# The second expert stage: both inner tiles of a step in one run, the last step's second product in one run, and two blocks' input split on another engine

## The chip, the core and the metric

The kernel runs on one core of a Trainium2 chip. The core has five engines with a queue each: TensorE (PE; matmuls, with the loads of the stationary operand shown apart as PEld), VectorE (DVE), ScalarE (ACT), GpSimd (POOL), and SyncE (SP), which here issues the DMAs. An engine works through its own queue in order and waits on semaphores for the others. The metric is the device time of one execution in microseconds (us), as the median over runs.

## What is computed

Three parts follow one another: a decayed linear attention, a mixture of eight experts, and a dense layer with a cosine gate. The change touches the third, for 3072 tokens of width 384 and an inner width of 2048:

```python
def _moe2_ref(x, w_in, w_out):
    h = x @ w_in
    g = h * np.cos(h)
    return (g @ w_out).astype(np.float32)
```

`x` is what the experts put out. The kernel treats the dense layer as a second expert stage.

## The kernel before

The tokens are cut into six blocks of 512 (`tb` 0 to 5). The inner widths are cut into units of 256: 32 units for the eight experts (`u` 0 to 31) and eight for the dense layer (`u` 32 to 39). A **step** is one unit on one block; the outer loop runs over units, the inner one over blocks. A unit has two inner tiles of 128 (`f` 0 and 1).

For precision every operand is held as a rounded high part and the rest: `xh`, `xl` for the input, `wh`, `wl` for the weights, `hh`, `hl` for the inner activations. A product is then three matmuls (`three`, lines 294 to 297): high by high, high by low, low by high.

A step has a first product for each inner tile (`g1`: nine matmuls of 512 columns, "wide") and a second product. In the dense layer the second product (`g2`) makes four token tiles of 128 by 384, six matmuls of 384 columns ("narrow") each. In the first stage it is transposed (`g2T`) and made of wide matmuls too.

Between the products of the dense layer stands `cos_split`, for each inner tile: ACT writes an Identity with an added constant (line 320), DVE subtracts (321), ACT does Sin (324) and Square (325), DVE multiplies (`g`, 328), ACT rounds to `hh` (331), POOL subtracts to `hl` (332). The scratch of these operations is called `raw` in the trace. The last two are put into a list, `late`, and taken out by the next tile's `cos_split` between its subtraction and its Sin.

The order of TensorE's work is written out by hand. `step` makes one tile's first product, then takes one entry off the list `g2q`, which holds second products in halves of two token tiles. With `lag=1` in the dense layer one entry stays in the list, so that TensorE alternates there: nine wide, twelve narrow, nine wide, twelve narrow. `one` advances a step by a quarter, and ahead of each quarter it advances the weight conversion (`wq`) and the input split (`xq`) by a piece.

`to_moe2` turns the experts' result of a block into the dense layer's input, in three pieces: ACT scales (662) and rounds to `xh` (663), POOL subtracts to `xl` (664). Blocks 0 to 3 are done in the last unit of the first stage, blocks 4 and 5 in steps 0 and 2 of unit 32. In that unit ACT also evacuates the second products (346); in the later ones DVE does (348). `ps` are the PSUM buffers: three rotate for first products, five for second ones.

Of the kernel before, what the change touches and what calls it, by code (L numbers as in the profile page):

```python
# [9 lines left out]
F32 = mybir.dt.float32  # L10
# [4 lines left out]
ALU = mybir.AluOpType  # L15
# [15 lines left out]
NU1 = E * UPE  # L31
NU2 = FF2 // FU
NU = NU1 + NU2
# [4 lines left out]
NTB = NT // TB  # L38
# [172 lines left out]
def body(tc, ap, t, fast, branch=None):  # L211
    nc = tc.nc
    te, act, dve, pool, sp = nc.tensor, nc.scalar, nc.vector, nc.gpsimd, nc.sync
    acc, accT, P, xh, xl = t.acc, t.accT, t.P, t.xh, t.xl
    wq, xq, gq = deque(), deque(), deque()

    class Ring:
        def __init__(self, items):
            self.items, self.n = list(items), 0
# [61 lines left out]
    def weight_tasks(u, loaded=False):  # L281
        if not loaded:
            load_w(u, 0)
            load_w(u, 1)
            yield
            for _ in range(1 if u < NU1 else 4):
                yield
        for i in range(NWP):
            yield from split_w(u, i)
            if 1 < u < NU1:  # L290
                yield


    def three(ps, ah, al, bh, bl, first, last):
        te.matmul(ps, ah, bh, start=first, stop=False)  # L295
        te.matmul(ps, ah, bl, start=False, stop=False)  # L296
        te.matmul(ps, al, bh, start=False, stop=last)  # L297
# [3 lines left out]
    def relu_split(e, tb, ps, hh, hl):  # L301
        if e:
            h = hring32.next()
            dve.scalar_tensor_tensor(out=h, in0=ps, scalar=0.0, in1=t.pb[tb], op0=ALU.max, op1=ALU.mult)  # L304
            act.activation(out=hh, in_=h, func=AF.Copy)  # L305

            def rest():
                dve.tensor_tensor(out=hl, in0=h, in1=hh.bitcast(F32), op=ALU.subtract)  # L308

            return rest  # L310
        act.activation(out=hh, in_=ps, func=AF.Relu)
        dve.scalar_tensor_tensor(out=hl, in0=ps, scalar=0.0, in1=hh.bitcast(F32), op0=ALU.max, op1=ALU.subtract)

    tring = Ring([t.raw[i][:, j * TB:(j + 1) * TB] for i in range(2) for j in range(2)])
    late = deque()

    def cos_split(ps, hh, hl):

        f = tring.next()
        act.activation(out=f, in_=ps, func=AF.Identity, bias=t.magic)  # L320
        dve.scalar_tensor_tensor(out=f, in0=f, scalar=MAGIC, in1=ps, op0=ALU.subtract, op1=ALU.subtract)  # L321
        if late:
            late.popleft()()
        act.activation(out=f, in_=f, func=AF.Sin, scale=math.pi)  # L324
        act.activation(out=f, in_=f, func=AF.Square)

        def g():
            dve.scalar_tensor_tensor(out=f, in0=f, scalar=0.5, in1=ps, op0=ALU.subtract, op1=ALU.mult)

        def split(last=False):  # L330
            act.activation(out=hh, in_=f, func=AF.Copy)  # L331
            (dve if last else pool).tensor_tensor(out=hl, in0=f, in1=hh.bitcast(F32), op=ALU.subtract)  # L332

        late.append(split)
        return g

    def evacT(u, tb, k, ps):
        a = accT[tb][:, k]
        if u == 0:
            act.activation(out=a, in_=ps, func=AF.Copy)  # L340
        else:
            dve.tensor_tensor(out=a, in0=ps, in1=a, op=ALU.add)  # L342

    def evac(u, tt, ps):
        if u == NU1:
            act.activation(out=acc[tt], in_=ps, func=AF.Copy, scale=TWO_PI)
            return
        dve.scalar_tensor_tensor(out=acc[tt], in0=ps, scalar=TWO_PI, in1=acc[tt], op0=ALU.mult, op1=ALU.add)
        if u == NU - 1:
            sp.dma_start(out=ap["out"][tt * 128:(tt + 1) * 128, :], in_=acc[tt])  # L350
# [3 lines left out]
    g2q = deque()  # L354

    def g1(u, tb, f):
        assert (u, 1) in wdone
        wh, wl = t.wh[u % 2], t.wl[u % 2]
        hh, hl = hid[u, tb, f] = hring.next()
        ps = ps1.next()  # L360
        for k in range(KT):
            o = k * FU + f * 128
            three(ps, wh[:, o:o + 128], wl[:, o:o + 128], xh[tb][:, k], xl[tb][:, k], k == 0, k == KT - 1)
        if u < NU1:
            return relu_split(u // UPE, tb, ps, hh, hl)
        return cos_split(ps, hh, hl)

    def g2_part(u, tb, i, f, ps):
        assert (u, 3) in wdone
        wh, wl = t.wh[u % 2], t.wl[u % 2]  # L370
        s = slice(i * 128, (i + 1) * 128)
        hh, hl = hid[u, tb, f]
        o = KT * FU + f * DM
        three(ps, hh[:, s], hl[:, s], wh[:, o:o + DM], wl[:, o:o + DM], f == 0, f == 1)

    def g2T(u, tb, k):
        assert (u, 3) in wdone
        wh, wl = t.wh[u % 2], t.wl[u % 2]
        ps = ps2.next()
        for f in range(2):  # L380
            hh, hl = hid[u, tb, f]
            o = KT * FU + f * DM + k * 128
            three(ps, wh[:, o:o + 128], wl[:, o:o + 128], hh, hl, f == 0, f == 1)
        evacT(u, tb, k, ps)

    def g2(u, tb, i):
        ps = ps2.next()[:, 0:DM]
        for f in range(2):
            g2_part(u, tb, i, f, ps)
        evac(u, tb * TPB + i, ps)  # L390

    def load_pb(e, tb):
        row = (e * NTB + tb) * TPB
        sp.dma_start(
            out=t.pb0[tb] if e == 0 else t.pb[tb],
            in_=t.pT[row:row + TPB, :].rearrange("t p -> (t p)").partition_broadcast(128))

    def step(u, tb, lag=0):

        if u == UPE:  # L400
            assert not gq
            pool.tensor_tensor(
                out=accT[tb], in0=accT[tb],
                in1=t.pb0[tb].rearrange("p (o n) -> p o n", o=1).to_broadcast([128, KT, TB]), op=ALU.mult)
        for f in range(2):
            rest = g1(u, tb, f)
            if f == 1 and u >= UPE and (u + 1) % UPE == 0 and u + 1 < NU1:
                load_pb((u + 1) // UPE, tb)
            yield
            if len(g2q) > lag:  # L410
                a, b, ks = g2q.popleft()
                for k in ks:
                    (g2T if a < NU1 else g2)(a, b, k)
                    if rest and u < NU1:
                        rest = rest()
            if rest:
                rest()
            if f == 1:
                g2q.extend([(u, tb, (0,)), (u, tb, (1, 2))] if u < NU1 else [(u, tb, (0, 1)), (u, tb, (2, 3))])
            yield  # L420


# [231 lines left out]
            load_pb(1, tb)  # L654
            load_pb(0, tb)

    def to_moe2(tb):

        yield
        for k in range(KT):  # L660
            a = accT[tb][:, k]
            act.activation(out=a, in_=a, func=AF.Copy, scale=1.0 / TWO_PI)  # L662
            act.activation(out=xh[tb][:, k], in_=a, func=AF.Copy)
            pool.tensor_tensor(out=xl[tb][:, k], in0=a, in1=xh[tb][:, k].bitcast(F32), op=ALU.subtract)
            yield


    dense = deque()

    def pull(q):  # L670
        while q:
            try:
                next(q[0])
                return
            except StopIteration:
                q.popleft()

    class Step:
        def __init__(self, u, tb, lag=0):
            self.it, self.left, self.u = step(u, tb, lag), 4, u  # L680

    def one():

# [48 lines left out]
    for c in range(NCH):  # L732
# [27 lines left out]
        if c == 2:  # L760
            act.activation(out=t.gater[:, :, 0:E], in_=t.gate, func=AF.Copy)
            dve.tensor_tensor(
                out=t.gater[:, :, E:2 * E], in0=t.gate, in1=t.gater[:, :, 0:E].bitcast(F32), op=ALU.subtract)
# [11 lines left out]
    for u in range(2, NU):  # L775
        if u == UPE:
            while gq:
                pull(gq)
            ps1.items.append(X0)
            ps2.items.extend([X1, X2])  # L780
        for tb in range(NTB):
            if tb == (1 if u + 1 < NU1 else 0) and u + 1 < NU:
                wq.append(weight_tasks(u + 1))
            if u == NU1 - 1 and tb >= 2:
                xq.append(to_moe2(tb - 2))
            if u == NU1 and tb in (0, 2):
                xq.append(to_moe2(NTB - 2 + tb // 2))
            if u == NU1 and tb == 4:
                assert not xq
            dense.append(Step(u, tb, lag=1 if u >= NU1 else 0))  # L790
            while one():
                pass

    late.popleft()(True)
    u, tb, ks = g2q.popleft()
    while len(g2q) >= 2:
        for i in ks:
            g2(u, tb, i)
        u, tb, ks = g2q.popleft()
    last = [ps2.next()[:, 0:DM] for _ in range(TPB)]  # L800
    for f in range(2):
        for i in range(TPB):
# [90 lines left out]
```

## Time and profile before

| | us |
|---|---|
| median of 3 runs | 2107.65 (2105.99 to 2108.02) |
| profiled execution, its own time | 2106.08 |
| its span | 2104.2 |
| TensorE busy | 2083.2 (99%) |
| DVE, ACT, POOL busy | 1357.3, 659.3, 484.1 |
| granted TensorE clock, mean | 0.997 |

The span is the time from the first to the last instruction of the profiled execution, whose own time is 1.88 us longer. A busy TensorE is not TensorE at its peak: the profile models the ends of its matmuls, so the distance between their starts is the better measure of its rate. A timeline row gives the start, the duration, the engine, the source line, the operation with what it writes and reads, and, in square brackets, how long the engine stood idle before it and what released it.

### The profile page before, as it was taken

How to read it: one execution, taken by the hardware profiler on the slowest of the kernel's cores; microseconds unless marked ns; L12 is line 12 of the kernel's file. 1: busy time of each engine (PE TensorE's matmuls, PEld its weight loads, DVE VectorE, ACT ScalarE, POOL GpSimd, SP SyncE). 2: the span in 40 equal slices, each digit the busy share in tenths (PEclk: the TensorE clock that was granted, in tenths of full speed). 3: DMA queues.
4: the chain of work that ended last, by engine and by line, in shares of the span. 5: the costliest groups of instructions: out<-in, count | busy, mean ns of one | idle time of the engine just before them, and what ended most of it. 6: DMA issues, size and time to landing. Idle time of an engine off the chain costs nothing.

```text
span 2104.2 us, 27561 instructions
## 1 busy us (share of the span) xinstructions
PE 2083.2 (99%) x11007; PEld 1742.0 (83%) x11007; DVE 1357.3 (65%) x2114; ACT 659.3 (31%) x1234; POOL 484.1 (23%) x428
## 2 busy tenths in 40 slices
PE   7999999999999999999999999999999999999998
PEld 6777788888888888888888888888888889999997
DVE  8553556666666666666666666666666867777775
ACT  4553211111111111111111121111111386666664
POOL 8872123000100000000000000000000264444442
PEclk9999999999999999999999999999999999999999
DMA  7441020001000100110010001001100011111102
GB/s 234 135 146 37 23 77 16 16 16 45 19 19 26 42 16 8 36 33 16 8 53 16 16 23 45 16 16 31 38 15 23 23 31 31 31 31 31 34 21 92
DMA packets 44458, 83.31 MB, mean 40 GB/s; under 512 B 5216, under 2 KB 28320, under 8 KB 44320
## 3 DMA queue, kind: packets, MB, share of 16 engines
q1 hardware_dynamic: 44320, 81.46, 12.7%
q8 instruction: 88, 1.44, 0.3%
q14 instruction: 50, 0.41, 0.1%
HBM read 76.63 MB, written 4.82 MB: 39 GB/s over the span
## 4 chain that ended last, share of the span: by engine, by line
PE 96%; ACT 1%; DVE 1%; DMA 1%; POOL 0%; issue 0%; SPq 0%; DVEq 0%; POOLq 0%; ACTq 0%
PE ps L295 31%; PE ps L297 31%; PE ps L296 31%; PE ps L499 1%; PE ps L540 1%; PE ps L548 1%; DMA raw<-in_rkT_dram 1%; PE ps L566 0%; DMA st<-in_wpk_dram 0%; PE ps L594 0%; PE ps L595 0%; ACT raw L320 0%; DVE raw L321 0%; ACT raw L324 0%; ACT acc L662 0%
## 5 line engine op out<-in xcount | busy, mean ns | idle before, releaser
L295 PE MATMUL ps<-xh,wh 128*128 128x512 f32 x1440 | 563.9, 392 | 0.0
L297 PE MATMUL ps<-xh,wl 128*128 128x512 f32 x1440 | 562.4, 391 | 0.0
L296 PE MATMUL ps<-xl,wh 128*128 128x512 f32 x1440 | 562.1, 390 | 0.0
L305 ACT ACTIVATE hh<-v 128x512 fp32r<-128x512 f32 x336 | 212.3, 632 | 1101.7 <-DVE v L304 1101.7
L342 DVE TENSOR_TENSOR acc<-ps,acc 128x512 f32<-128x512 f32 x558 | 384.6, 690 | 244.6 <-PE ps L297 236.6
L295 PE MATMUL ps<-hh,wh 128*128 128x512 f32 x1152 | 450.3, 391 | 0.0
L297 PE MATMUL ps<-hh,wl 128*128 128x512 f32 x1152 | 448.4, 389 | 0.0
L296 PE MATMUL ps<-hl,wh 128*128 128x512 f32 x1152 | 448.4, 389 | 0.0
L273 POOL TENSOR_TENSOR wl<-st,wh 128x384 fp32r<-128x384 f32 x120 | 122.0, 1017 | 1284.0 <-ACT wh L272 1267.3
L304 DVE SCALAR_TENSOR_TENSOR v<-ps,raw 128x512 f32<-128x512 f32 x336 | 232.3, 691 | 267.6 <-PE ps L297 267.6
L308 DVE TENSOR_TENSOR hl<-v,hh 128x512 fp32r<-128x512 f32 x336 | 319.0, 949 | 0.4 <-ACT hh L305 0.3
L295 PEld LDWEIGHTS ps<-xh,wh 128*128 128x128 f32 x1440 | 270.3, 188 | 57.1 <-issue 3.0
L297 PEld LDWEIGHTS ps<-xh,wl 128*128 128x128 f32 x1440 | 270.2, 188 | 56.9
L296 PEld LDWEIGHTS ps<-xl,wh 128*128 128x128 f32 x1440 | 270.3, 188 | 53.2
L295 PEld LDWEIGHTS ps<-hh,wh 128*128 128x128 f32 x1152 | 216.2, 188 | 45.7
L297 PEld LDWEIGHTS ps<-hh,wl 128*128 128x128 f32 x1152 | 216.2, 188 | 45.1
L296 PEld LDWEIGHTS ps<-hl,wh 128*128 128x128 f32 x1152 | 216.2, 188 | 44.7 <-DVE hl L308 0.2
L332 POOL TENSOR_TENSOR hl<-raw,hh 128x512 fp32r<-128x512 f32 x95 | 140.8, 1482 | 191.0 <-ACT hh L331 97.3
L297 PE MATMUL ps<-wh,hl 128*128 128x384 f32 x384 | 129.7, 338 | 2.2 <-POOL hl L332 2.2
L295 PE MATMUL ps<-wh,hh 128*128 128x384 f32 x384 | 129.5, 337 | 0.0
L296 PE MATMUL ps<-wl,hh 128*128 128x384 f32 x384 | 129.0, 336 | 0.0
L321 DVE SCALAR_TENSOR_TENSOR raw<-raw,ps 128x512 f32<-128x512 f32 x96 | 66.0, 688 | 76.7 <-ACT raw L320 76.6
(147 smaller groups left out, 1549.9 us busy)
## 6 DMA issues: line engine op xcount, KB each, us to landing
st<-in_wpk_dram SPq DMA_DIRECT2D x128, 192.0 KB, 2.4
AM<-in_wpk_dram SPq DMA_DIRECT2D x32, 384.0 KB, 3.0
raw<-pT SPq DMA_DIRECT2D x42, 256.0 KB, 3.3
raw<-in_rkT_dram SPq DMA_DIRECT2D x21, 448.0 KB, 4.0
kr<-in_kr_dram SPq DMA_DIRECT2D x21, 384.0 KB, 3.5
v<-in_v_dram SPq DMA_DIRECT2D x21, 224.0 KB, 3.8
out_dram<-acc SPq DMA_DIRECT2D x24, 192.0 KB, 1.9
acc<-in_rkT_dram SPq DMA_DIRECT2D x3, 448.0 KB, 5.5
```

Source lines behind the costliest of these rows:

```text
L273: (dve if u < 2 else pool).tensor_tensor(out=wl[:, s], in0=src, in1=wh[:, s].bitcast(F32), op=ALU.subtract)
L295: te.matmul(ps, ah, bh, start=first, stop=False)
L296: te.matmul(ps, ah, bl, start=False, stop=False)
L297: te.matmul(ps, al, bh, start=False, stop=last)
L304: dve.scalar_tensor_tensor(out=h, in0=ps, scalar=0.0, in1=t.pb[tb], op0=ALU.max, op1=ALU.mult)
L305: act.activation(out=hh, in_=h, func=AF.Copy)
L308: dve.tensor_tensor(out=hl, in0=h, in1=hh.bitcast(F32), op=ALU.subtract)
L321: dve.scalar_tensor_tensor(out=f, in0=f, scalar=MAGIC, in1=ps, op0=ALU.subtract, op1=ALU.subtract)
L332: (dve if last else pool).tensor_tensor(out=hl, in0=f, in1=hh.bitcast(F32), op=ALU.subtract)
L342: dve.tensor_tensor(out=a, in0=ps, in1=a, op=ALU.add)
L499: te.matmul(sc[i][:, j], k[q, j], r[q, j], start=True, stop=True)
L540: te.matmul(y[b % 4 * 32:b % 4 * 32 + 32, b // 4], t.v[buf(c)][:, VP * j + a:VP * j + a + 32], am(c, 2 * j + odd), start=i < 4, stop=False ...
```

## The change

In the dense layer a step is now made by `step2`: both first products one behind the other, then the whole second product of the step before, in two halves. `late` is emptied by the step itself between the halves, so its `hh` and `hl` are emitted there; in the very last step they come after the loop, as before. The two pieces that were left in `g2q` at the end are now one. `to_moe2` takes an engine; for blocks 4 and 5 it is DVE in place of POOL. `step`, now for the first stage alone, loses its `lag`.

```diff
-    def step(u, tb, lag=0):
+    def step2(u, tb):
+
+        rest = g1(u, tb, 0)
+        yield
+        rest()
+        rest = g1(u, tb, 1)
+        yield
+        for i in range(2):
+            if i and (u, tb) != (NU - 1, NTB - 1):
+                late.popleft()()
+            a, b, ks = g2q.popleft()
+            for k in ks:
+                (g2T if a < NU1 else g2)(a, b, k)
+            if i == 0:
+                rest()
+            else:
+                g2q.extend([(u, tb, (0, 1)), (u, tb, (2, 3))])
+            yield
+
+    def step(u, tb):
...
-            if len(g2q) > lag:
+            if g2q:
...
-    def to_moe2(tb):
+    def to_moe2(tb, en=pool):
...
-            pool.tensor_tensor(out=xl[tb][:, k], in0=a, in1=xh[tb][:, k].bitcast(F32), op=ALU.subtract)
+            en.tensor_tensor(out=xl[tb][:, k], in0=a, in1=xh[tb][:, k].bitcast(F32), op=ALU.subtract)
...
-            self.it, self.left, self.u = step(u, tb, lag), 4, u
+            self.it, self.left, self.u = (step if u < NU1 else step2)(u, tb), 4, u
...
-                xq.append(to_moe2(NTB - 2 + tb // 2))
+                xq.append(to_moe2(NTB - 2 + tb // 2, dve))
...
-            dense.append(Step(u, tb, lag=1 if u >= NU1 else 0))
+            dense.append(Step(u, tb))
...
-    u, tb, ks = g2q.popleft()
-    while len(g2q) >= 2:
-        for i in ks:
-            g2(u, tb, i)
-        u, tb, ks = g2q.popleft()
+    u, tb, _ = g2q.popleft()
```

Three places in the engines' queues, before and after. In these rows `ps_125`, `ps_126` and `ps_130` are the first products' PSUM buffers, `raw_103` and `raw_104` the scratch, `hh_95` and `hh_97` the two tiles of one step, `acc_87` and `xh_75` block 4, `acc_88` and `xh_76` block 5. Behind the change the lines 662 to 664 are 681 to 683.

ACT before, from step 0 of unit 32 on:

```order
L320 ACTIVATE raw_103<-ps_125,magic 128x512
L324 ACT_TABLE_LOAD
L324 ACTIVATE raw_103<-raw_103 128x512
L325 ACTIVATE raw_103<-raw_103 128x512
L662 ACTIVATE acc_87<-acc_87 128x512
L663 ACTIVATE xh_75<-acc_87 128x512
L662 ACTIVATE acc_87<-acc_87 128x512
L663 ACTIVATE xh_75<-acc_87 128x512
L320 ACTIVATE raw_103<-ps_126,magic 128x512
```

ACT after, from the second tile of the same step on:

```order
L320 ACTIVATE raw_103<-ps_126,magic 128x512
L331 ACTIVATE hh_95<-raw_103 128x512
L324 ACTIVATE raw_103<-raw_103 128x512
L325 ACTIVATE raw_103<-raw_103 128x512
L681 ACTIVATE acc_87<-acc_87 128x512
L682 ACTIVATE xh_75<-acc_87 128x512
L681 ACTIVATE acc_87<-acc_87 128x512
L682 ACTIVATE xh_75<-acc_87 128x512
L331 ACTIVATE hh_97<-raw_103 128x512
```

Before, two scale-and-round pairs stood ahead of the second tile's Identity; now one stands ahead of it, and two stand between its Square and its `hh`.

DVE before, at the same place:

```order
L321 SCALAR_TENSOR_TENSOR raw_103<-raw_103,ps_125 128x512
L342 TENSOR_TENSOR acc_88<-ps_131,acc_88 128x512
L328 SCALAR_TENSOR_TENSOR raw_103<-raw_103,ps_125 128x512
L321 SCALAR_TENSOR_TENSOR raw_103<-raw_103,ps_126 128x512
L328 SCALAR_TENSOR_TENSOR raw_103<-raw_103,ps_126 128x512
```

DVE after:

```order
L321 SCALAR_TENSOR_TENSOR raw_103<-raw_103,ps_125 128x512
L683 TENSOR_TENSOR xl_81<-acc_87,xh_75 128x512
L328 SCALAR_TENSOR_TENSOR raw_103<-raw_103,ps_125 128x512
L321 SCALAR_TENSOR_TENSOR raw_103<-raw_103,ps_126 128x512
L683 TENSOR_TENSOR xl_81<-acc_87,xh_75 128x512
L342 TENSOR_TENSOR acc_88<-ps_131,acc_88 128x512
L328 SCALAR_TENSOR_TENSOR raw_103<-raw_103,ps_126 128x512
```

Ahead of each tile's last operation (328) there now stands an `xl` of block 4, which reads what ACT rounds.

ACT after, from the second tile of step 2 of unit 32 on:

```order
L320 ACTIVATE raw_103<-ps_130,magic 128x512
L331 ACTIVATE hh_95<-raw_103 128x512
L324 ACTIVATE raw_103<-raw_103 128x512
L325 ACTIVATE raw_103<-raw_103 128x512
L681 ACTIVATE acc_88<-acc_88 128x512
L682 ACTIVATE xh_76<-acc_88 128x512
L346 ACTIVATE acc_84<-ps_127 128x384
L346 ACTIVATE acc_84<-ps_128 128x384
L681 ACTIVATE acc_88<-acc_88 128x512
L682 ACTIVATE xh_76<-acc_88 128x512
L331 ACTIVATE hh_97<-raw_103 128x512
```

ACT before, the same stretch:

```order
L320 ACTIVATE raw_103<-ps_130,magic 128x512
L331 ACTIVATE hh_95<-raw_103 128x512
L324 ACTIVATE raw_103<-raw_103 128x512
L325 ACTIVATE raw_103<-raw_103 128x512
L662 ACTIVATE acc_88<-acc_88 128x512
L663 ACTIVATE xh_76<-acc_88 128x512
L346 ACTIVATE acc_84<-ps_127 128x384
L346 ACTIVATE acc_84<-ps_128 128x384
L320 ACTIVATE raw_104<-ps_125,magic 128x512
```

Before, the second tile's `hh` followed the next step's Identity; now it follows the last pair of block 5.

## Rows read from the trace of the kernel before

**Rows 1.** First page: busy us (share of span) and instructions of each engine.

```profile
PE 2083.2 (99%) x11007; PEld 1742.0 (83%) x11007; DVE 1357.3 (65%) x2114; ACT 659.3 (31%) x1234; POOL 484.1 (23%) x428
```

**Rows 2.** TensorE's waits from 300 us on: us in total, times, longest.

```profile
PE ps L297 <- POOL hl L332: 2.2, 2, 1.2
```

**Rows 3.** TensorE's timeline: start us, duration us, engine, line, operation; first place.

```profile
1700.88 0.34 PE L297 MATMUL ps<-wh,hl 128*128 128x384 f32 x1
...
1702.79 0.44 PE L297 MATMUL ps<-wh,hl 128*128 128x384 f32 x1 [1.01 <-POOL hl L332]
1703.07 0.33 PE L295 MATMUL ps<-wh,hh 128*128 128x384 f32 x1
```

**Rows 4.** TensorE's timeline, second place.

```profile
1719.10 0.34 PE L297 MATMUL ps<-wh,hl 128*128 128x384 f32 x1
...
1721.49 0.34 PE L295 MATMUL ps<-wh,hh 128*128 128x384 f32 x1
```

**Rows 5.** ACT's timeline in unit 32, steps 0 to 2.

```profile
1694.39 0.63 ACT L663 ACTIVATE xh<-acc 128x512 fp32r<-128x512 f32 x1
...
1695.58 0.64 ACT L663 ACTIVATE xh<-acc 128x512 fp32r<-128x512 f32 x1
1696.11 0.67 ACT L320 ACTIVATE raw<-ps,magic 128x512 f32<-128x512 f32 x1
...
1700.50 0.62 ACT L331 ACTIVATE hh<-raw 128x512 fp32r<-128x512 f32 x1
...
1717.41 0.47 ACT L346 ACTIVATE acc<-ps 128x384 f32<-128x384 f32 x1
...
1718.72 0.64 ACT L331 ACTIVATE hh<-raw 128x512 fp32r<-128x512 f32 x1
```

**Rows 6.** DVE's timeline at the change of stage.

```profile
1686.00 0.68 DVE L308 TENSOR_TENSOR hl<-v,hh 128x512 fp32r<-128x512 f32 x1
...
1689.72 1.19 DVE L308 TENSOR_TENSOR hl<-v,hh 128x512 fp32r<-128x512 f32 x1
...
1693.87 0.69 DVE L328 SCALAR_TENSOR_TENSOR raw<-raw,ps 128x512 f32<-128x512 f32 x1 [1.16 <-ACT raw L325]
```

**Rows 7.** POOL's timeline: the `hl` that end the two stalls.

```profile
1701.34 1.40 POOL L332 TENSOR_TENSOR hl<-raw,hh 128x512 fp32r<-128x512 f32 x1
...
1719.49 1.66 POOL L332 TENSOR_TENSOR hl<-raw,hh 128x512 fp32r<-128x512 f32 x1 [0.36 <-POOL xl L664]
```

**Rows 8.** TensorE's timeline: the first matmuls of runs of one form.

```profile
1683.49 0.40 PE L295 MATMUL ps<-xh,wh 128*128 128x512 f32 x1
...
1685.58 0.39 PE L295 MATMUL ps<-hh,wh 128*128 128x512 f32 x1
...
1688.30 0.39 PE L295 MATMUL ps<-xh,wh 128*128 128x512 f32 x1
...
1691.70 0.39 PE L295 MATMUL ps<-xh,wh 128*128 128x512 f32 x1
...
1695.78 0.39 PE L295 MATMUL ps<-hh,wh 128*128 128x512 f32 x1
...
1730.90 0.39 PE L295 MATMUL ps<-xh,wh 128*128 128x512 f32 x1
...
2061.65 0.39 PE L295 MATMUL ps<-xh,wh 128*128 128x512 f32 x1
...
2063.73 0.33 PE L295 MATMUL ps<-wh,hh 128*128 128x384 f32 x1
...
2089.92 0.33 PE L295 MATMUL ps<-wh,hh 128*128 128x384 f32 x1
...
2093.04 0.33 PE L295 MATMUL ps<-wh,hh 128*128 128x384 f32 x1
```

**Rows 9.** Stretches: length, busy us (count) of each engine, granted clock, DMA share, GB/s.

```profile
26.70:30.10 3.40, 3.40 (x60) 2.62 (x60) 2.70 (x5) 0.16 (x1) 2.91 (x3) 0.50 0.59 163
1718.60:1722.00 3.40, 2.23 (x11) 1.56 (x10) 2.11 (x4) 3.14 (x8) 2.19 (x2) 1.00 0.36 116
```

More of the change, by code (lines that the diff above doesn't have):

```diff
@@ L409, in step @@
             yield
-            if len(g2q) > lag:
+            if g2q:
                 a, b, ks = g2q.popleft()
                 for k in ks:
-                    (g2T if a < NU1 else g2)(a, b, k)
-                    if rest and u < NU1:
+                    g2T(a, b, k)
+                    if rest:
                         rest = rest()
@@ L418, in step @@
             if f == 1:
-                g2q.extend([(u, tb, (0,)), (u, tb, (1, 2))] if u < NU1 else [(u, tb, (0, 1)), (u, tb, (2, 3))])
+                g2q.extend([(u, tb, (0,)), (u, tb, (1, 2))])
             yield
@@ L678, in body, with __init__ @@
     class Step:
-        def __init__(self, u, tb, lag=0):
-            self.it, self.left, self.u = step(u, tb, lag), 4, u
+        def __init__(self, u, tb):
+            self.it, self.left, self.u = (step if u < NU1 else step2)(u, tb), 4, u
     def one():
```

## The prediction

> **What bounds the kernel now.** The first page says TensorE: 2083.2 of 2104.2 us, 99% of the span [rows 1]. A 2% change in another engine is worth nothing unless TensorE waits for it, so I asked for TensorE's waits from 300 us to the end. There is one line: two matmuls waited for POOL, 2.2 us in all [rows 2]. Both lie in the first unit of the second expert stage. I then read TensorE's own timeline there, and ACT, DVE and POOL beside it, and last the distance from one matmul's start to the next, since an engine that never idles can still run slower than its best.
>
> The first stall is in the third matmul pair of a second product [rows 3]. From 1700.88 to 1703.07 four matmuls start, 2.19 us. An undisturbed 384-column matmul takes (2093.04 - 2089.92) / 18 = 0.173 us [rows 8], so 4 × 0.173 = 0.69 and 1.50 us are lost. In the second place four matmuls take 1721.49 - 1719.10 = 2.39 us [rows 4], so 1.70 are lost. Together **3.2 us** of waiting. The last tile's copy `hh` began on ACT at 1700.50 and 1718.72 [rows 5], and POOL's `hl` behind it at 1701.34 and 1719.49 for 1.40 and 1.66 us [rows 7]; each stall ends as POOL's `hl` does.
>
> The second loss is pitch. Eighteen 512-column matmuls in a row took 1695.78 - 1691.70 = 4.08 us, 0.227 each. In the steady part a half step is 9 matmuls of 512 columns and 12 of 384, which would be 2.04 + 2.08 = 4.12 us. From 1730.90 to 2061.65 there are 79 half steps, 330.75 us, 4.187 each [rows 8]. The excess is 0.067 us a half step. Of it 2063.73 - 2061.65 - 2.04 = 0.04 lies in the wide run, the rest, 0.027, in the narrow one.
>
> **The change part by part.**
>
> *The grouping.* The 24 narrow matmuls of a step's second product now stand together, and so do the 18 wide ones; their numbers stay. Where does the 0.067 belong? Two stretches tell me. After the short hitch ahead of 1683.49, nine wide matmuls took 2.09 us, 0.05 too long, and the next twelve wide ones 1688.30 - 1685.58 = 2.72, which is 12 × 0.227, undisturbed. And in the long narrow run of the tail the matmuls from the seventh on take 0.173 [rows 8]. So the excess looks like a price for each change of form, paid in the first six to ten matmuls after it. Half the changes go away: of some 91 entries into a wide run 46 stay, and of 92 into a narrow run 47. That is 45 × 0.04 + 45 × 0.027 = **3.0 us saved**. If the excess belongs to every wide matmul that follows a narrow run, however many, only the 45 × 0.027 = 1.2 us are saved; if it has to do with what the other engines read at that moment, 0. I take 3.0, since the twelve clean matmuls after the hitch are the nearest row.
>
> The Trainium skill ("TensorE: Matmul & The Clock Gate", section "Back-to-back issue gap") speaks against this term: it gives the gap between matmuls from the column count alone, so regrouping would save 0. The trace already disagrees with the plain rule, since the same 512 columns take 0.227 us in one place and 0.231 (2.08 / 9) in another; by the Trainium skill the whole sum below would be +1.9.
>
> *DVE splits blocks 4 and 5, and step 0 of the stage.* Here I follow the new queue order on the old clock. Up to ACT's first Identity nothing moves. ACT then scales and rounds the first piece of block 4, ending at 1694.39 + 0.63 = 1695.02 [rows 5]. On DVE the new `xl` stands **ahead of** the first tile's last operation (`g`), which had run at 1693.87 [rows 6]. DVE is in order, so `g` now waits for ACT: `xl` 1695.05 to 1695.7 (a two-input DVE operation on 512 columns, 0.68 [rows 6]), `g` to about 1696.4, the second tile's subtraction to 1697.0. ACT's second Identity comes earlier than before (about 1694.9 instead of 1696.11), but the gain is spent: `hh` of tile 0 ends near 1697.0, Sin and Square near 1698.3, and then come two whole scale-and-round pairs, 2 × 1.19 us (the step from 1694.39 to 1695.58), to about 1700.6. On DVE the second `xl`, an evacuation and only then `g` of tile 1: about 1701.4. `hh` of tile 1 ends near 1702.0, POOL's `hl` near 1703.4.
>
> TensorE has the same number of matmuls ahead of the second product as before, so it arrives at 1700.54 again and wants tile 1 after three matmuls, at 1701.06. It waits 1.0 us for `hh`, about 0.1 to get going, 0.9 for `hl`, 0.1 again: **2.1 us, where 1.5 were lost**.
>
> *Step 2 of the stage.* The first stall and its queue leave ACT late: its Identity for step 2 starts about 1710.6. From there to `hh` of tile 1 ACT's queue has: Identity, Sin, Square, a pair, Identity, `hh`, Sin, Square, a pair, two evacuation copies (0.47 each), a pair, `hh`. Before, two of the three pairs stood ahead of tile 1's Identity. With 0.53 to 0.65 us from start to start, and one gap of about 0.75 after each Identity while DVE works, `hh` of tile 1 ends near 1721.4 and `hl` near 1722.8. TensorE, 2.1 us late, wants them at 1719.6 and some 0.35 later: 1.8 + 0.1 + 1.0 + 0.1 = **3.0 us, where 1.7 were lost**.
>
> Together 5.1 against 3.2, **1.9 us added**. Bounds: if the `hl` of POOL takes 1.66 rather than 1.30 to 1.40 and one `xl` on DVE takes the 1.19 us of its nearest slow neighbour [rows 6, 7], 2 × 0.3 + 2 × 0.5 more, +3.5; if the chain is so much quicker than I walked it that nothing waits, -3.2.
>
> The Trainium skill ("SBUF — State Buffer", section "Who interferes with whom") says that a DVE operation with two SBUF inputs and a GpSimd operation that reads SBUF block each other. The trace agrees in that the same `hl` subtraction takes 0.68 and 1.19 us. By the Trainium skill the six `xl` would be slowed where POOL is at an `hl`; in my walk only the last pair touch, so it would add about 0.2 us.
>
> *The rest of the stage costs nothing in my sum.* In a steady step, walked in the same way (two chains of Identity, subtraction, Sin, Square, `g`, `hh` one behind the other, then `hl`), the `hl` of tile 1 is ready about 8.3 us after tile 0's last matmul, and TensorE asks for it after the second tile's 9 wide, 24 narrow, 18 wide and 5 narrow matmuls, 2.04 + 4.16 + 4.08 + 0.87 = 11.1 us. That cover of nearly 3 us is what hides the longer ACT and DVE chain; without it each of the 46 steps would pay. The scratch of the inner products rotates over three PSUM buffers and comes free 5 us ahead. The weight conversion keeps its places per quarter step, and the list of DMA issues on SP is unchanged. In the tail the last `hl` now stands behind two evacuations on DVE, but the first half of the last product, 12 × 0.173 = 2.1 us, covers one 0.68 us operation.
>
> **Sum.** +1.9 - 3.0 = -1.1 us. The profiled execution took 2106.08 us, 1.88 more than its span, so it would become 2105.0. The median of the runs shown is 1.57 us above the profiled one; on it the forecast is 2107.65 - 1.1 = **2106.5 us**. About 0.2%, 4.2 us, is what a measurement of this kernel can tell from no change, so this is no difference that can be measured.
>
> **The rivals.**
> *The stalls vanish.* This is the change as it reads: POOL is freed of six subtractions and TensorE gets 4 us more ahead of each second product. For it: POOL's `xl` stood right ahead of `hl` at 1719.49 [rows 7]. Against it: both stalls first wait for ACT's `hh`, and the walk moves that later. It gives -3.2 - 3.0, 2101.4 us. Chance 0.09.
> *The order does not touch the pitch*, or only the narrow runs': the excess follows the wide matmuls or the reads of other engines. For it: all nine matmuls of a wide run share the excess, and no row shows where a longer one recovers behind a narrow run. Stalls +1.9, pitch 0 to -1.2: 2108.4 to 2109.5 us. Chance 0.20. The Trainium skill's rule on the gap, named above, would give the upper of these two times.
> *The longer wait costs clock.* In 26.70 to 30.10 us TensorE was granted 0.50 (1.2 GHz of 2.4) after a thin stretch, while around the second stall it held 1.00 [rows 9]. A step-2 wait of 3 us, of which TensorE stands 1.8 in one piece, could be the point from which it falls. One such stretch of 3.4 us at half speed costs 1.7 us, one behind each stall 3.4. With no pitch gain: 2107.65 + 1.9 + 3.4 = 2113.0 us, slower. Against it: the present waits of 1.2 to 1.3 us did nothing to the clock. Chance 0.05.
>
> **How the numbers follow.** Forecast 0.66, the rivals 0.09, 0.20, 0.05. The forecast's own spread (+3.5 to 0 on the stalls, -3.0 to -1.2 on the pitch) and the second rival stay within 4.2 us of the old time. Faster by over 0.2% is the first rival and a sliver of the forecast: 0.10. Slower by over 0.2% is the third: 0.05. The range is 2103.7 to 2110.2: it leaves out the first rival and the third.
>
> **What would show it.** TensorE's waits should still name the first unit's second products in steps 0 and 2, now with ACT's `hh` first, about 2.1 and 3.0 us. DVE should show `g` waiting behind `xl`. A wide run of 18 after a narrow one should take about 4.12 us, its second half 2.04, and a narrow run of 24 about 4.19. A stall in any later unit, a narrow run whose pitch grows beyond the twelfth matmul, or a granted clock under 1.00 would make it wrong; so would stalls that are gone.

## The result and the profile after

The changed kernel takes **2129.7 us** (median; 2128.41 to 2134.05) against 2107.65 for the kernel before: 1.0102 times as long, interval 1.009 to 1.0115. It is 22 us slower. The forecast was 2106.5 us with a range up to 2110.2, so it was wrong, and on the wrong side.

The first page of the kernel after shows little of it. TensorE is still busy for 98% of the span, where it was 99% [rows 1], and the instruction count of TensorE is the same:

```profile
PE 2090.9 (98%) x11007; PEld 1743.6 (82%) x11007; DVE 1395.2 (66%) x2120; ACT 660.3 (31%) x1234; POOL 462.1 (22%) x422
```

One number stands out: DVE is busy for 1395.2 us instead of 1357.3, with six instructions more. Six subtractions of 0.7 us are 4 us, not 38.

TensorE's waits of the kernel after, from 300 us on (us in total, times, longest), had one line before, with two waits [rows 2]:

```profile
PE ps L297 <- POOL hl L332: 9.7, 14, 1.2
PE ps L295 <- ACT hh L331: 4.7, 6, 2.0
PE ps L296 <- POOL wl L273: 2.1, 2, 1.5
PE ps L295 <- ACT wh L272: 1.2, 2, 0.9
```

Twenty-four waits instead of two; four of them are for the weights' own `wh` and `wl`, which the conversion on DVE feeds. Since a wait also costs what TensorE needs to get going again, I took the distances between the starts of the stage's 2034 matmuls, from the first one of unit 32 to the last one. Each distance less the undisturbed 0.227 us (512 columns) or 0.173 (384) is put under pitch where it is below 0.04 us, and under stalls otherwise; a stretch at half clock counts with the stalls. The program's start varies by several us from one execution to the next (the first matmul of unit 32 starts at 1688.30 us in the profile of the kernel before and at 1696.63 in that of e7_both), so the stage is the better measure of a trace. For all kernels run (us; the undisturbed part is 399.4 in each; a ratio goes by the runs of the kernel before on the same chip):

| kernel | timed median | ratio to before | stage | pitch | stalls, unit 32 | stalls, units 33 to 39 |
|---|---|---|---|---|---|---|
| before | 2107.65 | | 408.8 | 6.1 | 3.2 | 0.1 |
| after | 2129.7 | 1.0102 [1.009, 1.0115] | 431.0 | 3.05 | 7.4 | 21.1 |
| e1_group_only | 2128.02 | 1.0085 [1.0063, 1.0107] | 430.5 | 3.2 | 3.6 | 24.3 |
| e2_split_only | 2110.72 | 1.0008 [0.9996, 1.0021] | 411.2 | 6.1 | 5.6 | 0.1 |
| e3_no_conv | 2107.73 | 0.9997 [0.9985, 1.0008] | 408.6 | 3.1 | 6.2 | 0 |
| e4_psum_ops | 2106.14 | 0.9991 [0.998, 1.0002] | 409.6 | 3.1 | 7.1 | 0 |
| e4c_ring4 | 2131.01 | 1.0118 [1.0095, 1.0141] | 430.6 | 3.1 | 8.5 | 19.6 |
| e5_rest_first | 2151.21 | 1.0197 [1.0177, 1.0217] | 452.1 | 3.0 | 7.5 | 42.2 |
| e6_conv_moved | 2109.14 | 1.0005 [0.9994, 1.0016] | 410.7 | 3.0 | 8.1 | 0.2 |
| e7_both | 2104.01 | 0.9981 [0.997, 0.9993] | 404.9 | 3.1 | 2.2 | 0.15 |
| e8_one_piece | 2109.39 | 0.9996 [0.9985, 1.0008] | 410.7 | 3.1 | 8.2 | 0 |
| e9_rest_conv | 2144.31 | 1.018 [1.0155, 1.0204] | 445.5 | 3.0 | 7.1 | 35.9 |
| e10_three | 2146.76 | 1.019 [1.0164, 1.0216] | 446.4 | 2.8 | 8.0 | 36.1 |

The first two rows settle where the 22 us come from: 3.06 are gained in pitch, 4.2 lost in unit 32, and **21 lost in units 33 to 39**, of which the prediction said that they cost nothing.

How does such a wait come about? TensorE's timeline of the kernel after, in unit 33 (start, duration, operation, idle time and releaser), from the start of a narrow run on:

```profile
1783.73 0.33 PE L295 MATMUL ps<-wh,hh 128*128 128x384 f32 x1
...
1787.91 0.39 PE L295 MATMUL ps<-xh,wh 128*128 128x512 f32 x1
...
1789.99 0.39 PE L295 MATMUL ps<-xh,wh 128*128 128x512 f32 x1
...
1792.03 0.33 PE L295 MATMUL ps<-wh,hh 128*128 128x384 f32 x1
...
1793.97 0.44 PE L297 MATMUL ps<-wh,hl 128*128 128x384 f32 x1 [0.79 <-POOL hl L332]
```

The narrow run to 1787.91 is clean, and the wide run behind it too. The next narrow run needs the second tile's `hl` and waits. Who made that late? DVE in the same stretch (x2 are two instructions behind one another):

```profile
1787.00 0.69 DVE L328 SCALAR_TENSOR_TENSOR raw<-raw,ps 128x512 f32<-128x512 f32 x1 [1.09 <-ACT raw L325]
1787.60 0.68 DVE L321 SCALAR_TENSOR_TENSOR raw<-raw,ps 128x512 f32<-128x512 f32 x1
1788.20 0.55 DVE L254 SCALAR_TENSOR_TENSOR kr<-AM,kr 128x384 int32<-128x384 int32 x1
1788.67 1.65 DVE L257 SCALAR_TENSOR_TENSOR kr<-AM,kr 128x384 f32<-128x384 uint32 x1
1790.24 1.01 DVE L348 SCALAR_TENSOR_TENSOR acc<-ps,acc 128x384 f32<-128x384 f32 x2
1791.18 0.67 DVE L328 SCALAR_TENSOR_TENSOR raw<-raw,ps 128x512 f32<-128x512 f32 x1
```

and POOL and ACT beside it:

```profile
1788.48 1.42 POOL L332 TENSOR_TENSOR hl<-raw,hh 128x512 fp32r<-128x512 f32 x1 [4.06 <-ACT hh L331]
...
1792.64 1.27 POOL L332 TENSOR_TENSOR hl<-raw,hh 128x512 fp32r<-128x512 f32 x1 [2.74 <-issue]
```

```profile
1791.88 0.63 ACT L331 ACTIVATE hh<-raw 128x512 fp32r<-128x512 f32 x1 [2.27 <-DVE raw L328]
```

Line 257 is a piece of the weight conversion. It began 0.19 us after POOL had begun the first tile's `hl`, and it ended at 1790.32, 0.42 us after POOL did (1788.48 + 1.42 = 1789.90). The piece before it, begun ahead of POOL, took 0.55. Behind the held piece stand two evacuations (348) and the second tile's last DVE operation (328). ACT waited 2.27 us for that one, POOL's `hl` came at 1792.64 to 1793.91, and TensorE, which wanted it at 1793.0, stood. This step had begun late already; how one step's delay comes to the next is told further below.

In the kernel before, the same two engines overlap there too, but the other way round. DVE's and POOL's rows of the kernel before:

```profile
1789.00 0.55 DVE L254 SCALAR_TENSOR_TENSOR kr<-AM,kr 128x384 int32<-128x384 int32 x1
```

```profile
1789.01 1.70 POOL L332 TENSOR_TENSOR hl<-raw,hh 128x512 fp32r<-128x512 f32 x1 [2.69 <-ACT hh L331]
```

DVE began 0.01 us earlier, kept its 0.55, and POOL's `hl` took 1.70 instead of the 1.27 of the row above. POOL had the time; DVE in the new order has not.

The groups by line from 1724 us on (the end of unit 32 and units 33 to 39) show that this is the rule. First the kernel after (line, instructions | busy us, mean ns | idle before), then the one before:

```profile
L328 DVE SCALAR_TENSOR_TENSOR raw<-raw,ps 128x512 f32<-128x512 f32 x88 | 60.1, 683 | 54.7 <-ACT raw L325 54.7
...
L257 DVE SCALAR_TENSOR_TENSOR kr<-AM,kr 128x384 f32<-128x384 uint32 x27 | 22.8, 845 | 0.0
...
L254 DVE SCALAR_TENSOR_TENSOR kr<-AM,kr 128x384 int32<-128x384 int32 x26 | 21.8, 840 | 0.3
L246 DVE TENSOR_SCALAR kr<-AM 128x384 int32<-128x384 int32 x26 | 18.2, 701 | 0.0
...
L244 DVE TENSOR_SCALAR kr<-AM 128x384 int32<-128x384 int32 x26 | 16.7, 642 | 0.0
```

```profile
L328 DVE SCALAR_TENSOR_TENSOR raw<-raw,ps 128x512 f32<-128x512 f32 x89 | 61.2, 687 | 19.0 <-ACT raw L325 19.0
...
L244 DVE TENSOR_SCALAR kr<-AM 128x384 int32<-128x384 int32 x25 | 18.4, 735 | 0.0
...
L254 DVE SCALAR_TENSOR_TENSOR kr<-AM,kr 128x384 int32<-128x384 int32 x26 | 14.4, 554 | 0.3
L257 DVE SCALAR_TENSOR_TENSOR kr<-AM,kr 128x384 f32<-128x384 uint32 x26 | 14.3, 551 | 0.0
...
L246 DVE TENSOR_SCALAR kr<-AM 128x384 int32<-128x384 int32 x25 | 8.8, 352 | 0.0
```

Six of the conversion's seven operations got slower by half or more; the seventh (244) was held in the kernel before already, 735 against 642 ns. The operations that read PSUM did not (328, 687 and 683 ns). Over the stage's 196 pieces the time above the undisturbed 0.35 or 0.55 us is 12 us before (15 pieces held by over 0.2 us) and 56 us after (63 held). Before, 17 of the pieces began while POOL was at an operation; after, 73 did, and 71 of these were held by over 0.1 us. Of those that began while POOL stood, none was, in either kernel.

### The profile page after: what moved, and what is told of

It is laid out like the page before. It is cut to its first block, busy times and chain, and to the rows that moved or that the text cites. A ratio compares the mean times of both kernels' runs of the same rounds, so it can differ in the third digit from the quotient of the medians.

```text
span 2126.7 us, 27555 instructions
## 1 busy us (share of the span) xinstructions
PE 2090.9 (98%) x11007; PEld 1743.6 (82%) x11007; DVE 1395.2 (66%) x2120; ACT 660.3 (31%) x1234; POOL 462.1 (22%) x422
## 4 chain that ended last, share of the span: by engine, by line
PE 80%; DVE 14%; ACT 5%; issue 1%; DMA 0%; DVEq 0%; ACTq 0%
PE ps L295 26%; PE ps L297 25%; PE ps L296 25%; DVE acc L348 3%; DVE raw L328 2%; DVE raw L321 2%; ACT raw L324 1%; ACT raw L325 1%; PE ps L518 1%; PE ps L559 1%; DVE kr L254 1%; DVE kr L257 1%; DVE kr L261 1%; DVE kr L252 1%; PE ps L567 1%
## 5 line engine op out<-in xcount | busy, mean ns | idle before, releaser
L332 POOL TENSOR_TENSOR hl<-raw,hh 128x512 fp32r<-128x512 f32 x95 | 126.8, 1335 | 240.5 <-ACT hh L331 129.6
```

## The experiments

Theory A: a conversion piece on DVE that begins while POOL works on `hl` or `wl` is held until POOL is done, and what stands behind it in DVE's queue makes the second tile late. Theory B: DVE's queue holds too much work ahead of the second tile's last operation, whatever POOL does. Theory C: the split of blocks 4 and 5 on DVE does it.

**Each half of the change alone.** The grouping, with the split left on POOL:

```diff
-                xq.append(to_moe2(NTB - 2 + tb // 2, dve))
+                xq.append(to_moe2(NTB - 2 + tb // 2))
```

> Only the grouping of the matmuls; the last blocks' split is back on POOL. Theory A (the weight conversion on DVE meets POOL's hl and wl, waits until POOL's operation ends, and DVE's whole queue runs late): the stalls of units 33 to 39, some 21 us, stay; 2120 to 2130 us. Theory B (DVE has too much work in its queue ahead of the second tile's last operation, whether or not it meets POOL): the same. Theory C (the split on DVE in unit 32 throws everything out of step): the stalls go; about 2105 us.

2128.02 us: nearly the whole loss, with 24.3 us of stalls in units 33 to 39. The reverse, the kernel before with the split on DVE (`to_moe2` with the engine as an argument, `dve` for blocks 4 and 5):

> Only the split of blocks 4 and 5 on DVE; the order of the kernel before. A and B: units 33 to 39 without a stall as before, unit 32 loses 3 to 6 us in place of 3.2; 2107 to 2111 us. C: some 20 us slower than before, about 2128 us.

2110.72 us, with no stall behind unit 32. C is out as a cause of the 21 us. The split does cost in unit 32: 7.4 against 3.6 us with the new order, 5.6 against 3.2 with the old one.

**The conversion left out, or made without a second operand from SBUF.** The first kernel leaves the conversions of units 33 to 39 out:

```diff
-            yield from from_f64(i, i >= NWP // 2)
+            if u == NU1:
+                yield from from_f64(i, i >= NWP // 2)
+            else:
+                for _ in range(7):
+                    yield
```

> The changed kernel without the seven DVE operations that convert a weight piece, from unit 33's weights on (the places in the order stay empty, the piece is rounded from old numbers). A and B: units 33 to 39 have no stall, unit 32's 4 to 7 us are left, the 3 us of pitch are gained; 2108 to 2112 us. C: no change from the changed kernel, about 2130 us.

2107.73 us, no stall in units 33 to 39. The second puts seven other operations of the same width into their places, each with one operand in PSUM:

```diff
+    def psum_ops(i):
+
+        e, w, p = cv[0], cv[3 + i % 2], X2[:, 0:WP]
+        for n in range(7):
+            o = w if n == 6 else e
+            dve.scalar_tensor_tensor(out=o, in0=p, scalar=1.0, in1=e, op0=ALU.mult, op1=ALU.mult)
+            yield
...
+                yield from psum_ops(i)
...
+        if u == NU1:
+            ps2.items, ps2.n = [t.ps[3], t.ps[4], X1, t.ps[2]], 0
```

> The changed kernel, where from unit 33's weights on seven DVE operations of 128x384 with one input in PSUM stand in place of the conversion (so four PSUM buffers rotate for the second products, not five). They take 7 x 0.55 = 3.9 us a piece, the conversion's undisturbed sum is 3.1 us. A: operations that never meet POOL at the SBUF port cost no stall though they are longer; units 33 to 39 lose under 3 us; 2108 to 2113 us. B: more work in the same places, so at least the 21 us of stalls of the changed kernel; 2130 us or more.

2106.14 us, and again no stall in units 33 to 39. (Both kernels came out slightly below the ranges expected of theory A.) Its group by line from 1724 us on:

```profile
L270 DVE SCALAR_TENSOR_TENSOR kr<-ps,kr 128x384 f32<-128x384 f32 x183 | 101.0, 552 | 2.5
```

All of them took 0.54 to 0.56 us, though undisturbed pieces of the conversion take 0.35 to 0.55: more DVE work at rest, at the same places, and nothing waits. B falls. One thing differed besides, the four PSUM buffers of the second product, so these went alone into the changed kernel:

> A control for e4_psum_ops: the changed kernel as it is, with its weight conversion, and only with the four PSUM buffers for the second product that e4_psum_ops also had. Theory A (the conversion on DVE meets POOL's operations on SBUF): the buffers do nothing, the time stays that of the changed kernel, 2129 us (2126 to 2133), with about 20 us of TensorE waits in units 33 to 39. Rival R (it was the rotation of the PSUM buffers, not the operands in PSUM, that freed e4_psum_ops of its waits): 2106 us (2104 to 2109) and no waits there.

2131.01 us, as the changed kernel. It was the operands.

**The second tile's operation ahead of the evacuations.** If two evacuations and a held piece stand in front of 328, putting 328 ahead of the evacuations should help:

```diff
             a, b, ks = g2q.popleft()
+            if i == 0:
+                rest()
             for k in ks:
                 (g2T if a < NU1 else g2)(a, b, k)
             if i == 0:
-                rest()
+                pass
```

> The changed kernel, with the last two operations of the second inner tile (DVE's subtraction L328 and what follows it) written ahead of the first two evacuations of the second product, so that fewer DVE operations stand between the conversion and the operation that TensorE waits for. Theory A: a conversion that is held by POOL still delays DVE, by less than before what TensorE has in hand, and about half of the waits in units 33 to 39 go: 2117 us (2113 to 2121). Rival Q (the place of that one subtraction behind the evacuations is the whole cause): all waits of units 33 to 39 go, 2108 us (2105 to 2110). If DVE's queue has no part in it: 2129 us.

2151.21 us. Every expectation missed, theory A's too, and on the wrong side: stalls of units 33 to 39 doubled. I come back to it below.

**Where the pieces stand.** The changed kernel pulls 2, 1, 2, 1 pieces ahead of the four quarters of a step (the text on record of the next kernel names them the wrong way round). This one pulls 2, 3, 0, 1, so the two pieces ahead of the evacuations and 328 move to the quarter before:

```diff
-        for _ in range(1 + (s.left % 2 == 0 and s.u >= NU1 - 1)):
+        for _ in range({4: 2, 3: 3, 2: 0, 1: 1}[s.left] if s.u >= NU1 else 1 + (s.left % 2 == 0 and s.u >= NU1 - 1)):
```

> The changed kernel with its six conversion pieces of a step in other quarters: two in the first quarter of a step, three in the second, none in the third and one in the fourth, instead of 1, 2, 1, 2. Nothing is left out or added. Theory A: the pieces now mostly run where POOL has no operation, keep their 0.35 to 0.57 us, and the waits of units 33 to 39 go; unit 32 keeps its 5 to 7 us (the split of the last two blocks on DVE); 2107.5 us (2105 to 2110.5). Rival G (the grouping itself makes the second tile's hl late, wherever the conversion stands): 2125 us or more. Theory B (too much DVE work in the queue): the same amount of work, so 2120 us or more.

2109.14 us; the 21 us are gone with nothing left out. TensorE's waits from 300 us on are those of unit 32 alone:

```profile
PE ps L295 <- ACT hh L331: 2.7, 2, 1.8
PE ps L297 <- POOL hl L332: 1.7, 2, 0.9
```

But the pieces did not keep their durations, as A had said: 27 of the 56 us of held time remain, nearly all in pieces ahead of the next step's first subtraction (321). There it harms nobody. So being held is not enough; the place counts. Three kernels test that. With one piece in the third quarter (2, 2, 1, 1):

> The changed kernel with the conversion pieces of a step at 2, 2, 1, 1 over its four quarters; the changed kernel has 2, 1, 2, 1 and e6_conv_moved 2, 3, 0, 1 (the text for e6_conv_moved names the changed kernel's numbers the wrong way round). So one of the two pieces that stand in front of the evacuations and of the second tile's subtraction is moved to the quarter before. Theory P (what counts is how long DVE is held between the second tile's two subtractions, with a slack that one held piece of about 1.1 us just fits in): the waits of units 33 to 39 go below 2 us, as with none, and the time is 2108.5 us (2106 to 2112). Rival L (each piece there costs its share): about half of the 20 us stays, 2119 us (2115 to 2123).

2109.39 us, no stall. With three (2, 0, 3, 1):

> The pieces at 2, 0, 3, 1: three in front of the evacuations and of the second tile's subtraction where the changed kernel has two. Theory P: a third piece adds up to 1.1 us of held time in each of some 42 steps less the clear ones, waits of units 33 to 39 of 30 to 40 us, 2144 us (2137 to 2150). Rival L: half as much again as in the changed kernel, 2139 us; if the third quarter has no part in it, 2129 us.

2146.76 us. One, two and three pieces in that place give 0, 21 and 36 us of stalls. The jump is from one to two, and the reason is in the rows. DVE of the kernel with one piece, and POOL beside it:

```profile
1787.60 0.68 DVE L321 SCALAR_TENSOR_TENSOR raw<-raw,ps 128x512 f32<-128x512 f32 x1
1788.19 0.55 DVE L257 SCALAR_TENSOR_TENSOR kr<-AM,kr 128x384 f32<-128x384 uint32 x1
1788.66 1.01 DVE L348 SCALAR_TENSOR_TENSOR acc<-ps,acc 128x384 f32<-128x384 f32 x2
1789.64 0.69 DVE L328 SCALAR_TENSOR_TENSOR raw<-raw,ps 128x512 f32<-128x512 f32 x1
```

```profile
1788.47 1.43 POOL L332 TENSOR_TENSOR hl<-raw,hh 128x512 fp32r<-128x512 f32 x1 [4.05 <-ACT hh L331]
```

The single piece is on its way before POOL begins, and the evacuations behind it read PSUM and pass POOL freely. Line 257, which took 1.65 us at 1788.67, takes 0.55 at 1788.19. So my price (a slack that one held piece fits into) was beside the point: a first piece is not held there. In the changed kernel's units 33 to 39 none of the first pieces at this place was held and 22 of the 24 second ones were: a second one comes up to 0.5 us later, after POOL has begun. From 321 to 328 of the second tile a steady step takes 2.05 us before and with one piece or none, 2.78 in the changed kernel, and 3.16 with three pieces (means over 41 steps). The time that theory P named for three pieces came out, but not by its price of up to 1.1 us for a third held piece: the held time at this place goes only from 23 to 28 us, and the rest is the further pieces' own 0.35 to 0.55 us.

The last test was e5_rest_first with the pieces at 2, 3, 0, 1:

> e5_rest_first (2151 us) with the pieces at 2, 3, 0, 1 as in e6_conv_moved. Theory P: the two pieces ahead of the second tile's subtraction made e5_rest_first slow, not the place of the subtraction: no waits in units 33 to 39, 2109 us (2106 to 2112). Rival S (the subtraction ahead of the evacuations is itself harmful, by the later evacuations and by the fourth quarter's piece that now meets POOL): half or more of the 42 us of waits there stays, 2125 us or more.

2144.31 us: P misses, S holds. DVE of this kernel, with POOL:

```profile
1799.53 0.69 DVE L328 SCALAR_TENSOR_TENSOR raw<-raw,ps 128x512 f32<-128x512 f32 x1 [1.36 <-ACT raw L325]
1800.13 1.01 DVE L348 SCALAR_TENSOR_TENSOR acc<-ps,acc 128x384 f32<-128x384 f32 x2
1801.06 1.64 DVE L254 SCALAR_TENSOR_TENSOR kr<-AM,kr 128x384 int32<-128x384 int32 x1
1802.62 1.01 DVE L348 SCALAR_TENSOR_TENSOR acc<-ps,acc 128x384 f32<-128x384 f32 x2
...
1804.67 0.68 DVE L321 SCALAR_TENSOR_TENSOR raw<-raw,ps 128x512 f32<-128x512 f32 x1
```

```profile
1801.01 1.28 POOL L332 TENSOR_TENSOR hl<-raw,hh 128x512 fp32r<-128x512 f32 x1 [1.35 <-issue]
```

With 328 first, its own `hh` and `hl` follow at once, and POOL begins 1.48 us after 328 did. The fourth quarter's piece comes to DVE 1.53 us after 328, behind two evacuations: 0.05 us too late, and so in every step that has a piece there: all 28 pieces at this place took 1.08 to 1.11 us more than at rest, 30.6 us together. And four evacuations, not two, now stand between 328 and the next step's 321, which begins 5.14 us after it (mean 4.35; 3.35 in the changed kernel). So the next step's chain starts late from the outset. Which of the two, the held piece or the evacuations, weighs more was not separated.

**Both causes taken away.** The pieces at 2, 3, 0, 1, the split back on POOL, and its own pieces in the first and third quarter alone:

```diff
-        pull(xq)
+        if s.u != NU1 or s.left in (4, 2):
+            pull(xq)
...
-                xq.append(to_moe2(NTB - 2 + tb // 2, dve))
+                xq.append(to_moe2(NTB - 2 + (tb == 2)))
...
```

> As e6_conv_moved, and in unit 32 the split of blocks 4 and 5 is put back on POOL, with its pieces in the first and third quarter of a step alone. If the two causes found so far are all (conversion against POOL in units 33 to 39, the split on DVE in unit 32), the waits of the stage come to 2 to 3.5 us, no clock drop is left, and the pitch saving of 3.06 us remains: 2104.5 us (2102.5 to 2107), 1.5 to 3.5 us below the kernel before. If unit 32 stalls whatever the split does: 2107 to 2109 us, as e6_conv_moved.

2104.01 us, 0.9981 times the kernel before (0.997 to 0.9993): **a fifth of a per cent below the kernel before**, small but outside the interval. Its stage takes 404.9 us, 3.9 less than before: 3.0 of pitch and 0.9 of stalls. The remaining waits from 300 us on are one line:

```profile
PE ps L297 <- POOL hl L332: 1.3, 2, 0.8
```

## Why the prediction was wrong, point by point

**The pitch: right.** 3.0 us forecast, 3.06 measured (6.11 to 3.05), with the same in every kernel that has the new order and none in the one that has not. The runs look as described: eighteen wide matmuls from 1787.91 to 1792.03 take 4.12 us, the second nine of them 2.04 (from 1789.99), and the narrow run before them 4.18. So the excess is a price of each change of form, and the second rival, that the order does not touch the pitch, is out. The Trainium skill's rule ("TensorE: Matmul & The Clock Gate", section "Back-to-back issue gap"), by which regrouping saves 0, does not hold here.

**Step 0 of unit 32: right. Step 2: too small, and a rival beside it came true.** TensorE's timeline of the kernel after at the two places [rows 3, 4]:

```profile
1701.71 0.34 PE L297 MATMUL ps<-wh,hl 128*128 128x384 f32 x1
...
1704.56 0.34 PE L295 MATMUL ps<-wh,hh 128*128 128x384 f32 x1
...
1720.64 0.34 PE L297 MATMUL ps<-wh,hl 128*128 128x384 f32 x1
1723.01 0.44 PE L295 MATMUL ps<-wh,hh 128*128 128x384 f32 x1 [2.03 <-ACT hh L331]
...
1725.29 0.52 PE L295 MATMUL ps<-wh,hh 128*128 128x384 f32 x1
```

Four matmuls each: 2.85 - 0.69 = 2.2 us lost in step 0, 2.1 forecast; 4.65 - 0.69 = 4.0 in step 2, 3.0 forecast, `hh` first as forecast. Then the clock fell, and the rest of the 7.4 us (7.4 - 2.2 - 4.0 = 1.2) lies there. The windows of the kernel after (length, busy us and count of PE, PEld, DVE, ACT, POOL, granted clock, DMA share, GB/s), at this place and at a stall in unit 38:

```profile
1724.30:1727.70 3.40, 2.89 (x9) 2.89 (x10) 2.51 (x4) 1.84 (x3) 0.45 (x1) 0.50 0.36 111
2024.70:2028.10 3.40, 3.40 (x13) 3.40 (x12) 2.80 (x6) 2.44 (x5) 1.29 (x1) 0.50 0.03 7
```

The third rival named this place, this mechanism and 1.7 us a drop. Both together cost 3.0 us. It was right as a mechanism and far too small to decide the sign, since its time was made without the term below. The term for unit 32 came to +4.2 where +1.9 stood, outside its bound of +3.5.

**"The rest of the stage costs nothing": the step that failed.** It is 21 of the 22 us. The cover of nearly 3 us was worked out with every DVE operation at its undisturbed duration, and with the sentence that the weight conversion "keeps its places per quarter step". It does keep its quarters. But in the old order a quarter held one tile's work: pairs of pieces stood in front of a subtraction (321) that waited for ACT anyway, and between 321 and 328 stood one piece at most, never held in units 33 to 39. In the new order two pieces stand between the second tile's two subtractions, right where the first tile's `hl` goes to POOL.

The cover itself was right for a step without conversion. The rows of one step of e3_no_conv, TensorE's and POOL's (lines 295, 297 and 332 are 299, 301 and 336 there; the first row is the first matmul of the second tile, the second one the first to read its `hl`):

```profile
1781.30 0.39 PE L299 MATMUL ps<-xh,wh 128*128 128x512 f32 x1
...
1792.53 0.34 PE L301 MATMUL ps<-wh,hl 128*128 128x384 f32 x1
```

```profile
1788.47 1.29 POOL L336 TENSOR_TENSOR hl<-raw,hh 128x512 fp32r<-128x512 f32 x1 [1.36 <-issue]
```

The second tile's `hl` is ready 8.5 us after the first tile's last matmul (1788.47 + 1.29 - 1781.30; 8.3 in the walk), and TensorE takes it up after 11.2 (11.1 there). One hold of 1.1 us would fit into that. What the walk of a single step could not see is that the delay is handed on: in ACT's queue the second tile's `hh` stands ahead of the next step's Identity, and in DVE's queue the evacuations and the last quarter's piece stand ahead of its 321. Where a piece between 321 and 328 of the second tile was held, DVE of the changed kernel takes 9.5 us from a step's first 321 to the next step's (mean of 22 steps of units 33 to 39). TensorE's undisturbed step takes 8.31. So the delay adds up. In unit 35, steps 1 to 5, `hl` is ready 9.4, 9.4, 10.6, 11.1 and 12.7 us after that matmul, and TensorE stalls in the last one alone; the next unit's first step, with little conversion in it, wins most of it back. Over steps 1 to 5 of units 33 to 38 DVE's mean distance is 8.35 to 8.42 us in e4_psum_ops, e8_one_piece and e6_conv_moved, which have no stalls, and 9.16, 9.44, 9.49 and 9.65 in the changed kernel, e10_three, e9_rest_conv and e5_rest_first, which lose 21, 36, 36 and 42 us.

The rule was in the prediction. The Trainium skill ("SBUF — State Buffer", section "Who interferes with whom") has DVE operations with two SBUF inputs and GpSimd operations that read SBUF block each other, and says that "issue order, not op shape, decides who blocks". The runs agree: 0.55 us becomes 1.65 when DVE comes second, POOL's 1.27 becomes 1.70 when POOL does, and with an input in PSUM nothing changes (0.54 to 0.56). I applied it to the six `xl` that the diff shows, at 0.2 us, and not to the 196 pieces that the diff does not touch but moves against POOL. The trace before had the sign: in [rows 7] `hl` takes 1.40 and 1.66 us, above the undisturbed 1.27, and on DVE a piece of the conversion had begun just ahead of each. POOL was then the one that waited. DVE of the kernel before:

```profile
1701.23 0.37 DVE L249 TENSOR_SCALAR kr<-kr 128x384 int32<-128x384 int32 x1
...
1719.47 0.55 DVE L261 SCALAR_TENSOR_TENSOR kr<-kr,kr 128x384 f32<-128x384 f32 x1
```

**The stalls vanish: out.** They grew in unit 32. That POOL, freed of six subtractions, would help did not show: the split on DVE cost 3.8 us in the new order and 2.4 in the old.

**What would show it.** The list named "a stall in any later unit" as what would make the forecast wrong, and it did.

## What to carry to other kernels

When an order changes, price the work that keeps its place in the code too: list for each engine what now begins beside what, above all pairs on DVE and POOL that both read SBUF, and ask which of the two begins second and who waits behind it. A held operation costs only where something that TensorE needs stands behind it in the same queue. A cover worked out for one step is not enough, either: compare the time that each engine's queue takes for a whole step with the bottleneck's, since a longer one adds up from step to step. Moving a held operation by one place (one piece to the quarter before, as in e8_one_piece) can take the cost from 21 us to none. And when a queue is rearranged, check the far end as well: putting the awaited operation first moved the loss to the next step's start and doubled it.

## What the runs showed of the hardware

- A held DVE operation ends not with POOL's but later, by its own duration less some 0.14 us: 0.41 to 0.42 us for the operations of 0.55 (27 in the changed kernel, 1790.32 against 1789.90 among them), 0.21 to 0.22 for those of 0.35 (44). The integer operations with one input (246, 352 ns at rest, 701 in the mean) are held like those with two.
- A difference of hundredths of a microsecond decides who waits: 0.01 us ahead, and DVE keeps its 0.55; 0.05 us behind, and it takes 1.64.
- TensorE's granted clock went from 1.00 to 0.50 (2.4 to 1.2 GHz) behind the stalls of 4.0 us in unit 32 and some 2.3 us at 2021 of the changed kernel. In unit 32 it fell in every kernel that has both the new order and the split on DVE, and in no other. Behind stalls of 1.5 to 2.8 us in unit 32 of the kernel before, of e2_split_only and of the changed kernel's step 0 it stayed at 1.00; in e10_three it fell behind step 0, after the same two waits (1.0 and 0.9 us) as in the changed kernel. So the length of a stall alone does not order the cases. What does was not tried.
